# Gated attention and low-rank mixer: quartering the odd small matmuls, loads moved behind the first x + h's turn, scores over two PSUM tiles, other cover pairs, a last store in two

## The chip, the cores and the metric

One core of one Trainium2 chip. The metric is the device time of one execution in microseconds (us), as the median of several runs. The core has TensorE (PE, matrix products into PSUM), VectorE (DVE), ScalarE (ACT), GpSimd (POOL), and SyncE (SP), whose queue here issues all transfers. Each engine works through its instructions in the order in which they were written.

## What is computed

```python
batch, seq, d_model = (8, 3136, 256); d_qk = 64; rank = 32
# first part, for each batch
attn = np.maximum((1.0 / S) * np.matmul(z, z.transpose(0, 2, 1)), 0.0) ** 2
x = u * np.matmul(attn, v)
# second part
h = x.transpose(0, 2, 1) @ U @ V
u2 = x + h.transpose(0, 2, 1)
out = u2 + np.maximum(u2 @ w_ch1, 0.0) @ w_ch2        # w_ch1 256x1024, w_ch2 1024x256
```

## The kernel before, in words

The sequence of 3136 is cut into 24 full tiles of 128 rows and one of 64 (`NF` = 24, `NT` = 25). Full tiles come in six groups of four (512 rows, `NQ` = 6); the 64 rows are a seventh, small group (`NG` = 7). An item is a pair (batch, group); there are 56, and the loop over `t` gives each a slot. In slot `t` the attention of item `t` runs, x + h of the item seven back (`u2_unit`), and both layers of the item eight back (`ch1_part`, `ch2_stream`). `t == NG` is the slot of item (1, 0), the first in which the low-rank product of batch 0 (`t1_all`) and x + h occur.

All arithmetic of TensorE is in bfloat16 with float32 sums. The reduction of most products is cut into two halves of 64 rows, h = 0 and 1, that lie on the two halves of the array: `pair` (line 179) issues the two matmuls, each into another PSUM bank. A stream (`Ways`, line 616) does all its matmuls in one assignment of halves to banks, then in the other; between the two, `post` (line 170) has GpSimd hand on the semaphore that says that the other half has done with the bank. Line 184, the one in `pair`, therefore stands for nearly all matmuls in the profile. Four PSUM tiles of two banks each exist (`ps0` to `ps3`).

- Scores (`score_pairs`): z is held transposed twice over (`zzT`); two key tiles by 512 columns make a pair, rectified and squared into a block (`blk`). ScalarE mostly rectifies (L399) and VectorE squares (L364). Half of the blocks are mirror images, made by a transposing transfer (`issue_turn`, L421 and L429). At the very start the first two pairs (`rectify`, way "half", L376 to L381) are shared: ScalarE takes one bank, VectorE the other, of the same PSUM tile.
- The small group: `score_small`, and `av_small` (L714), the 64 rows' product with v on four quarters of the array, with 25 key tiles over two column halves. `t1_all` (L797) sums U times x over 25 tiles on four column strips of 32. `u2_unit` gives x + h; for the small group it is one matmul on half of the array.
- x + h is rounded to bfloat16 (L886) and turned by a transposing transfer (`x_turn`, L785) into `u2T`, which the first layer reads (L184, `ps<-u2T,w_bf`). The rectified result (L959 on VectorE, L962 on ScalarE) feeds the second layer (`ps<-w_bf,blk`).
- In the small group's slot there is no attention stream to fill waits. The second layer's stream runs in two halves, with score pairs or `av_small` between them as cover (`late`, line 1444).

The order of the work is planned in Python by a clock of its own (`clock`, `book`, `hold`, in units of a 256-column pair): `hold(due, f)` puts off loads, casts and squares, and `emit` (line 1110) mixes queues of units into a light stream, by places in that stream. SP issues transfers in the order planned; each also waits for the one eight before it. Loads of slot `t` (`load_part` for the next batch, `first_loads` for U, V and the two weights) are held to places in the slot up to `t == NG`; their casts run in the slot after it. `todo` spreads the score jobs over the slots. The last group's output is stored in two parts (`ch2_halves`, L1068, L1069).

Of the kernel before, what the change touches and what calls it, by code (L numbers as in the profile page):

```python
# [18 lines left out]
def kernel(  # L19
# [85 lines left out]
    ways = ["half", "half", "both", "dve"]  # L105
# [260 lines left out]
    def rectify(dst, src, b, part=1, whole=False):  # L366
# [3 lines left out]
        if whole and slot[0] == 0:  # L370
# [4 lines left out]
            if way == "half":  # L375
                nc.scalar.activation(out=dst[:, 0], in_=src[:, 0], func=AF.Relu, scale=scale)  # L376
                nc.vector.tensor_scalar(  # L377
                    out=dst[:, 1], in0=src[:, 1], scalar1=scale, scalar2=0.0, op0=ALU.mult, op1=ALU.max
                )
                nc.scalar.activation(out=dst[:, 0], in_=dst[:, 0], func=AF.Square)  # L380
                nc.vector.tensor_tensor(out=dst[:, 1], in0=dst[:, 1], in1=dst[:, 1], op=ALU.mult)  # L381
                done = max(book("act", ready, 5.2), book("dve", ready, 6.2))
                return done, max(book("act", ready, 5.2), book("dve", ready, 3.5))
# [156 lines left out]


# [161 lines left out]
    def av_small(b, g):  # L703
# [7 lines left out]
        for jt in range(NT):  # L711
            c = jt % 2
            for h in range(2):
                nc.tensor.matmul(  # L714
                    out=ps[c * hp : c * hp + rows, h, :D],
                    lhsT=smalls[b][h * hp : (h + 1) * hp, place_of(jt), :],
                    rhs=v_bfs[b][h * hp : (h + 1) * hp, jt, :],
                    start=(jt < 2),
                    stop=(jt >= NT - 2),
                    tile_position=(h * hp, c * hp),  # L720
                )
# [70 lines left out]
    def t1_all(b):  # L792
        k, pt = take_ps()
        for g in range(NG):
            for q, it, rows in tiles_of(g):
                c = it % NREP
                nc.tensor.matmul(  # L797
# [4 lines left out]
                    stop=(it + NREP >= NT),  # L802
                    tile_position=(0, c * R),
                )
        pe(8)
# [17 lines left out]
    def u2_unit(b, g, turn=True):  # L823
# [20 lines left out]
        else:  # L844
# [4 lines left out]
                        0,  # L849
                        0,  # L850
                        dict(
                            out=ps[:, 0, :D],
                            lhsT=V4_bf[:hp, t0 * P : (t0 + 1) * P],
                            rhs=t1s[b][:hp, :],
# [3 lines left out]
                    )  # L858
                ],
                D,  # L860
# [9 lines left out]
        nc.vector.tensor_tensor(out=o[:rows, :n, :], in0=four(ps)[:rows, :n, :], in1=x, op=ALU.add)  # L870
# [167 lines left out]
    def ch2_halves(b, g):  # L1038
# [3 lines left out]
        for a in range(2):  # L1042
            box = {}

            def step(i, way, first, least, a=a, box=box):
# [19 lines left out]
                if least == NH:  # L1065
                    ps_free[box["k"]] = book("dve", clock[0] + 3, 6.4)
                    o = u2s[b, g][:, 2 * a : 2 * a + 2, :]
                    nc.vector.tensor_tensor(out=o, in0=box["ps"][:, :, :D], in1=o, op=ALU.add)  # L1068
                    nc.sync.dma_start(out=rows_of(out[b])[:, g0 + 2 * a : g0 + 2 * a + 2, :], in_=o)  # L1069
                    queued(GW // 2)  # L1070
# [135 lines left out]
    def load_V(i0):  # L1206
# [30 lines left out]
        6: lambda: load_w(1),  # L1237
# [76 lines left out]
    score_burst(jobs0[:1])  # L1314
    score_burst(jobs0[1:2])
# [4 lines left out]
    for b in range(B):  # L1320
        for g in range(NQ):
            t = b * NG + g - 1
            new = jobs_of(b, g)
            if g == 0 and b > 0:
                x, y = (5, 10) if b == 1 else (5, 11)
# [18 lines left out]
    def early(b, g):  # L1344
        return b > 1 and g == NQ

    for t in range(n_items):
# [11 lines left out]
        if t > NG and g_now == NQ and b_next < B:  # L1359
            hold(clock[0] + 60 + 70, lambda b=b_next: load_u(b, NQ))  # L1360
        if t == n_items - 3:
            xTs[direct] = take_block()[1][:, : GT // 2, :].rearrange("p a (q d c) -> p (a q) d c", d=ND, c=P)
            x_turn(*direct, xTs[direct])
        for i, f in enumerate(casts_next):
            hold(clock[0] + (90 if g_now == NQ and b_next > 1 else 60 if t == NG else 15 if t >= NQ else 45) + 12 * i, f)
# [4 lines left out]
        steps += first_loads[t]() if t in first_loads else []  # L1370
# [4 lines left out]
        for i, f in enumerate(steps):  # L1375
            if t > NG:
                load(f)
            else:
                hold(clock[0] + 5 + 22 * i, lambda f=f: load(f))
        if t <= NG:  # L1380
            hold(clock[0] + 60, lambda t=t: load_u(*items[t + 1]))
# [35 lines left out]
        elif av:  # L1417

            if mix:
                qc += [(x, 1 - way, False, lambda way=way: ch1_small(*mix, way, box1)) for way, x in ((0, 36), (1, 48))]  # L1420
            if fin:
# [109 lines left out]
```

## Time and profile before

| | |
|---|---|
| Time, median of 3 runs | 983.55 us (982.08 to 983.84) |
| Profiled execution | 986.39 us, of it 984.6 from the first to the last instruction (span) |
| PE / DVE / ACT / POOL busy | 99% / 64% / 49% / 2% of the span |
| Granted TensorE clock, mean | 0.998 |
| DMA | 176.37 MB, 179 GB/s on the average |
| Chain that ended last | PE 96%, of it line 184 93% of the span; DMA of u2T 1% |

Each matmul row of the profile gives the start, the duration, the lines and the tiles; matmuls overlap, so the time from one start to the next is the slot that it takes, while its duration also holds its way through the array. "idle before <- releaser" is how long an engine stood and for whom. The granted clock is the share of full speed that TensorE was given.

### The profile page before, as it was taken

Reading aid. Unit: us, or ns where it says so; the run is one execution under the profiler, and the core shown is the slowest. Engines: PE = TensorE matmul, PEld = TensorE weight load, DVE = VectorE, ACT = ScalarE, POOL = GpSimd, SP = SyncE. Lnnn points to the kernel's source line nnn. Section 1 sums busy time; section 2 is a strip of 40 time slices with the busy share of each in tenths; the row PEclk is TensorE's granted clock in tenths of the full one; section 3 lists DMA queues with packets and bytes.
Section 4 is the critical chain, followed back from the end, with each engine's and each line's share of the span. In section 5 each row is a group of like instructions: output and inputs, shape, how many; then the busy total and the mean of one; then the engine's idle time right before and its main releaser. Section 6 shows DMA issues by size and latency. Waiting matters only on the chain.

```text
span 984.6 us, 35373 instructions
## 1 busy us (share of the span) xinstructions
PE 973.7 (99%) x16163; PEld 773.4 (79%) x16163; DVE 628.2 (64%) x811; ACT 482.4 (49%) x565; POOL 15.2 (2%) x25
## 2 busy tenths in 40 slices
PE   8999899999999999999999999999999999999998
PEld 5788677877778778787777877788777887778766
DVE  6878755668556685566755667556775567653363
ACT  7877642456324473355633555334654346431353
POOL 4200000000000000000000000000000000000000
PEclk9999999999999999999999999999999999999999
DMA  8899999979997799987999879997799978965153
GB/s 269 193 225 192 228 196 188 223 153 197 195 204 167 160 192 192 205 170 170 185 208 207 154 178 179 223 189 153 173 207 206 194 144 163 186 135 95 55 114 99
DMA packets 372405, 176.37 MB, mean 179 GB/s; under 512 B 347296, under 2 KB 350624, under 8 KB 372256
## 3 DMA queue, kind: packets, MB, share of 16 engines
q1 hardware_dynamic: 372256, 174.12, 85.6%
q8 instruction: 126, 2.06, 0.9%
q14 instruction: 23, 0.19, 0.1%
HBM read 62.56 MB, written 25.69 MB: 90 GB/s over the span
## 4 chain that ended last, share of the span: by engine, by line
PE 96%; DVE 1%; ACT 1%; DMA 1%; issue 0%; DVEq 0%
PE ps L184 93%; PE ps L714 1%; DMA u2T<-x_bf 1%; PE ps L797 1%; ACT blk L399 0%; PE ps L1096 0%; DVE blk L364 0%; PE ps L1300 0%; PE ps L331 0%; DVE blk L377 0%; DVE blk L381 0%; DVE x_bf L749 0%; DVE blk L406 0%; DVE out_sb L870 0%; DVE blk L395 0%
## 5 line engine op out<-in xcount | busy, mean ns | idle before, releaser
L184 PEld LDWEIGHTS <-blk 64*128 64x128 bf16 x12288 | 609.7, 94 | 159.9 <-POOLq L174 9.6
L184 PE MATMUL ps<-v_bf,blk 64*128 64x256 bf16 x9216 | 613.0, 269 | 2.3 <-DVE blk L364 1.1
L399 ACT ACTIVATE blk<-ps 128x1024 bf16<-128x1024 f32 (+1 forms) x335 | 315.3, 970 | 346.6 <-PE ps L184 343.2
L364 DVE TENSOR_TENSOR blk<-blk 128x1024 bf16<-128x1024 bf16 x350 | 221.1, 656 | 49.1 <-ACT blk L399 48.4
L184 PE MATMUL ps<-u2T,w_bf 64*128 64x512 bf16 (+1 forms) x1792 | 227.9, 350 | 2.8 <-DMA u2T<-x_bf 2.8
L184 PE MATMUL ps<-w_bf,blk 64*128 64x256 bf16 x3072 | 192.0, 269 | 0.0
L959 DVE TENSOR_SCALAR blk<-ps 128x1024 bf16<-128x1024 f32 x105 | 128.5, 1224 | 97.6 <-PE ps L184 96.6
L962 ACT ACTIVATE blk<-ps 128x1024 bf16<-128x1024 f32 x87 | 88.3, 1022 | 119.0 <-PE ps L184 118.8
L184 PE MATMUL ps<-zzT 64*128 64x512 bf16 (+2 forms) x902 | 129.8, 327 | 0.6 <-ACT zzT L340 0.6
L184 PEld LDWEIGHTS <-w_bf 64*128 64x128 bf16 x1792 | 84.3, 94 | 30.2 <-POOLq L174 5.0
L749 DVE TENSOR_TENSOR x_bf<-ps,u_sb 128x1024 bf16<-128x1024 f32 x48 | 58.7, 1222 | 71.4 <-PE ps L184 71.4
L870 DVE TENSOR_TENSOR out_sb<-ps,x_bf 128x1024 f32<-128x1024 f32 x42 | 51.4, 1224 | 58.1 <-PE ps L184 58.1
L1082 DVE TENSOR_TENSOR out_sb<-ps,out_sb 128x1024 f32<-128x1024 f32 x42 | 51.4, 1224 | 18.6 <-PE ps L184 18.3
L184 PEld LDWEIGHTS <-zzT 64*128 64x128 bf16 x902 | 41.2, 94 | 6.9 <-ACT zzT L340 1.5
L184 PE MATMUL ps<-t_sb,V_bf 64*128 64x256 bf16 x200 | 20.6, 269 | 0.0
L395 DVE TENSOR_SCALAR blk<-ps 128x1024 bf16<-128x1024 f32 (+1 forms) x14 | 16.6, 1185 | 5.9 <-PE ps L184 5.1
L206 DVE CAST v_bf<-stage 128x1024 bf16<-128x1024 f32 (+1 forms) x30 | 18.5, 617 | 0.0
L184 PE MATMUL ps<-v_bf,last_sb 64*128 64x256 bf16 x192 | 18.5, 269 | 0.0
L204 ACT CAST v_bf<-stage 128x1024 bf16<-128x1024 f32 (+1 forms) x18 | 18.1, 1005 | 0.0
L206 DVE CAST x_bf<-out_sb 128x1024 bf16<-128x1024 f32 x22 | 15.2, 689 | 0.3
L1082 DVE TENSOR_TENSOR blk<-ps,blk 128x1024 f32<-128x1024 f32 x5 | 6.1, 1225 | 11.9 <-PE ps L184 11.8
L204 ACT CAST x_bf<-out_sb 128x1024 bf16<-128x1024 f32 x13 | 13.5, 1037 | 0.0
(83 smaller groups left out, 239.1 us busy)
## 6 DMA issues: line engine op xcount, KB each, us to landing
u_sb<-in_u_dram SPq DMA_DIRECT2D x48, 512.0 KB, 5.1
stage<-in_v_dram SPq DMA_DIRECT2D x42, 512.0 KB, 6.1
out_dram<-out_sb SPq DMA_DIRECT2D x42, 512.0 KB, 3.1
stage<-in_z_dram SPq DMA_DIRECT2D x7, 512.0 KB, 5.9
blk<-in_v_dram SPq DMA_DIRECT2D x5, 512.0 KB, 6.3
out_dram<-blk SPq DMA_DIRECT2D x5, 512.0 KB, 2.6
blk<-blk SPq DMA_TRANSPOSE x156, 5.1
blk<-in_moe_w_ch_dram SPq DMA_DIRECT2D x4, 512.0 KB, 4.9
```

The costliest lines, as they stand in the source:

```text
L184: ins = nc.tensor.matmul(**args)
L204: nc.scalar.copy(out=out, in_=in_)
L206: nc.vector.tensor_copy(out=out, in_=in_)
L364: nc.vector.tensor_tensor(out=a, in0=a, in1=a, op=ALU.mult)
L395: nc.vector.tensor_scalar(out=dst, in0=src, scalar1=scale, scalar2=0.0, op0=ALU.mult, op1=ALU.max)
L399: nc.scalar.activation(out=dst, in_=src, func=AF.Relu, scale=scale)
L714: nc.tensor.matmul(out=ps[c * hp : c * hp + rows, h, :D], lhsT=smalls[b][h * hp : (h + 1) * hp, place_of(jt), :], rhs=v_bfs[b][h * hp : (h ...
L749: nc.vector.tensor_tensor(out=xs[b, g][:rows, :n, :], in0=four(box["ps"])[:rows, :n, :], in1=u_sbs[b, g][:rows, :n, :], op=ALU.mult,)
L870: nc.vector.tensor_tensor(out=o[:rows, :n, :], in0=four(ps)[:rows, :n, :], in1=x, op=ALU.add)
L959: nc.vector.tensor_single_scalar(out=r, in_=ps[:, :, :gw], scalar=0.0, op=ALU.max)
L962: nc.scalar.activation(out=r, in_=ps[:, :, :gw], func=AF.Relu)
L1082: nc.vector.tensor_tensor(out=o, in0=acc, in1=o, op=ALU.add)
```

## The change

Eight edits.

1. `av_small`: the 25th key tile is split by columns over both column halves: four matmuls of 128 columns instead of two of 256. `t1_all`: the 25th tile is split into four strips of 64 columns, one for each column strip of the array. `u2_unit`, small group: two matmuls of 128 columns on the two halves of the array instead of one of 256 on one half; the sum reads both banks.
2. The first two score pairs (`shared_pairs`) lie over two PSUM tiles, so that ScalarE reads only one and VectorE only the other.
3. Loads of the slots up to `t == NG`: U, V and weights ahead of the next batch's v; w2 is loaded in slot 7 instead of 6; at `t == NG` all loads are held to place 78 and later, and the next u to 88; at `t == NQ` the next u is loaded at place 5 instead of 60. So z of batch 2, w2 and u stand behind the first turn in SP's queue. Casts of the slot after follow at 45.
4. Batch 1's `av_small` is done in slot `NG`, at place 64, instead of as cover in slot 13; its u comes ahead for that.
5. Batches 2 to 7: two more of the first group's scores are left for the small slot.
6. Small slot: x + h of the small group comes first, then the first layer's eight parts, then a score pair; two score pairs, not one, lie between the halves of the second layer.
7. The last group's second store is split in two, the adds too; the second half goes out from ScalarE's queue.
8. Way "half" goes away.

```diff
...
     ready_turns = []
     urgent = []
     slot = [0]
-    ways = ["half", "half", "both", "dve"]
+    ways = ["both", "dve"]
     waiting = [0]
     def needed(e):
...
             ends = {"dve": dve + DVE, "act": act + 19, "both": max(act + 8.7, dve) + 7.5}
             given = bool(ways)
             way = ways.pop(0) if ways else min(ends, key=lambda w: ends[w])
-            if way == "half":
...
             if way == "dve":
                 if not given:
                     run_held(ready + 9)
...
         score_finish(score_pairs(jobs))
+    def shared_pairs(jobs):
+
+        (ka, a), (kb, d) = take_ps(), take_ps()
+        for i, (b, g, (J, h)) in enumerate(jobs):
+            zzT = zzTs[b]
+            if h == 0:
+                blocks[b, g, J] = take_block()
+            for jj in range(2):
+                key = J * GT + 2 * h + jj
+                nc.tensor.matmul(
+                    out=(a if jj == i else d)[:, jj, :],
+                    lhsT=half(zzT, jj, key * P, P),
+                    rhs=half(zzT, jj, groups[g][0], GW),
+                    start=True,
+                    stop=True,
+                )
+            pe(GW / 256)
+            dst = blocks[b, g, J][1][:, 2 * h : 2 * h + 2, :]
+            x, y = dst[:, i], dst[:, 1 - i]
+            nc.scalar.activation(out=x, in_=a[:, i], func=AF.Relu, scale=scale)
+            nc.vector.tensor_scalar(out=y, in0=d[:, 1 - i], scalar1=scale, scalar2=0.0, op0=ALU.mult, op1=ALU.max)
+            nc.scalar.activation(out=x, in_=x, func=AF.Square)
+            nc.vector.tensor_tensor(out=y, in0=y, in1=y, op=ALU.mult)
+            ps_free[ka] = book("act", clock[0] + 3, 5.2)
+            ps_free[kb] = book("dve", clock[0] + 3, 6.2)
+            book("act", 0, 5.2)
+            book("dve", 0, 3.5)
+
+            def finish(key=(b, g, J)):
+                squared[key] = squared.get(key, 0) + 1
+
+            hold(max(free_at["act"], free_at["dve"]), finish)
+
     def place_of(jt):
         if jt == NF:
...
         for jt in range(NQ + 1):
             while (b, jt) not in v_cast:
                 run_held(min(h[0] for h in held))
-        for jt in range(NT):
+        for jt in range(NT + 1):
             c = jt % 2
+            part = slice(0, D) if jt < NF else slice(c * D // 2, (c + 1) * D // 2)
+            at = min(jt, NF)
             for h in range(2):
                 nc.tensor.matmul(
-                    out=ps[c * hp : c * hp + rows, h, :D],
-                    lhsT=smalls[b][h * hp : (h + 1) * hp, place_of(jt), :],
-                    rhs=v_bfs[b][h * hp : (h + 1) * hp, jt, :],
+                    out=ps[c * hp : c * hp + rows, h, part],
+                    lhsT=smalls[b][h * hp : (h + 1) * hp, place_of(at), :],
+                    rhs=v_bfs[b][h * hp : (h + 1) * hp, at, part],
                     start=(jt < 2),
-                    stop=(jt >= NT - 2),
+                    stop=(jt >= NF),
                     tile_position=(h * hp, c * hp),
                 )
         pe(NT / 2 + 2)
...
         for g in range(NG):
             for q, it, rows in tiles_of(g):
                 c = it % NREP
+                if it == NF:
+                    break
                 nc.tensor.matmul(
                     out=pt[c * R : (c + 1) * R, 0, :D],
                     lhsT=U_bf[:, it, :],
                     rhs=xs[b, g][:, q, :],
                     start=(it < NREP),
-                    stop=(it + NREP >= NT),
+                    stop=False,
                     tile_position=(0, c * R),
                 )
-        pe(8)
+        for c in range(NREP):
+            part = slice(c * D // NREP, (c + 1) * D // NREP)
+            nc.tensor.matmul(
+                out=pt[c * R : (c + 1) * R, 0, part],
+                lhsT=U_bf[:, NF, :],
+                rhs=xs[b, NQ][:, 0, part],
+                start=False,
+                stop=True,
+                tile_position=(0, c * R),
+            )
+        pe(7)
         up = pool.tile([P, D], FP32, name="t1_up", bufs=1)
         t1 = pool.tile([P, D], BF16, name="t1_sb")
...
                 k,
                 [
                     (
-                        0,
-                        0,
+                        h,
+                        h,
                         dict(
-                            out=ps[:, 0, :D],
-                            lhsT=V4_bf[:hp, t0 * P : (t0 + 1) * P],
-                            rhs=t1s[b][:hp, :],
+                            out=ps[:, h, : D // 2],
+                            lhsT=V4_bf[h * hp : (h + 1) * hp, t0 * P : (t0 + 1) * P],
+                            rhs=t1s[b][h * hp : (h + 1) * hp, h * D // 2 : (h + 1) * D // 2],
                             start=True,
                             stop=True,
                         ),
                     )
+                    for h in range(2)
                 ],
-                D,
+                D // 2,
             )
         x = xs[b, g][:rows, :n, :]
         if b == B - 1:
...
         else:
             o = pool.tile([P, GT, D], FP32, name="out_sb", bufs=3)
         done = ps_free[k] = book("dve", clock[0] + 3, 11.2 * n / GT)
-        nc.vector.tensor_tensor(out=o[:rows, :n, :], in0=four(ps)[:rows, :n, :], in1=x, op=ALU.add)
+        if n == GT:
+            nc.vector.tensor_tensor(out=o, in0=four(ps), in1=x, op=ALU.add)
+        else:
+            apart = lambda a: a[:rows, 0, :].rearrange("p (c d) -> p c d", c=2)
+            nc.vector.tensor_tensor(out=apart(o), in0=ps[:rows, :, : D // 2], in1=apart(x), op=ALU.add)
         u2s[b, g] = o
         if not turn:
             return
...
                     post(box["k"])
                 if least == NH:
                     ps_free[box["k"]] = book("dve", clock[0] + 3, 6.4)
-                    o = u2s[b, g][:, 2 * a : 2 * a + 2, :]
-                    nc.vector.tensor_tensor(out=o, in0=box["ps"][:, :, :D], in1=o, op=ALU.add)
-                    nc.sync.dma_start(out=rows_of(out[b])[:, g0 + 2 * a : g0 + 2 * a + 2, :], in_=o)
+                    o = u2s[b, g]
+                    for q, n in ((0, 1), (1, 1)) if a else ((0, 2),):
+                        t = 2 * a + q
+                        nc.vector.tensor_tensor(
+                            out=o[:, t : t + n, :], in0=box["ps"][:, q : q + n, :D], in1=o[:, t : t + n, :], op=ALU.add
+                        )
+                        (nc.scalar if q else nc.sync).dma_start(
+                            out=rows_of(out[b])[:, g0 + t : g0 + t + n, :], in_=o[:, t : t + n, :]
+                        )
                     queued(GW // 2)
             units.append(Ways(NH, 0, step, box).units)
...
         3: lambda: load_V(0),
         4: lambda: load_V(2),
         5: lambda: load_w(0),
-        6: lambda: load_w(1),
+        NG: lambda: load_w(1),
     }
...
     clock[0] = 43
     free_at.update(dve=46, act=47)
     jobs0 = jobs_of(0, 0)
-    score_burst(jobs0[:1])
-    score_burst(jobs0[1:2])
+    shared_pairs(jobs0[:2])
     score_burst(jobs0[2:3])
     clock[0] = 60
...
             t = b * NG + g - 1
             new = jobs_of(b, g)
             if g == 0 and b > 0:
-                x, y = (5, 10) if b == 1 else (5, 11)
+                x, y = (5, 10) if b == 1 else (5, 9)
                 todo[t - 2] += new[:x]
                 todo[t - 1] += new[x:y]
                 todo[t] += new[y:12] if b == 1 else new[y:]
...
     direct = (B - 1, 0)
     def early(b, g):
-        return b > 1 and g == NQ
+        return b > 0 and g == NQ
     for t in range(n_items):
         slot[0] = t
...
             load_u(*items[t + 1])
         if t > NG and g_now == NQ and b_next < B:
             hold(clock[0] + 60 + 70, lambda b=b_next: load_u(b, NQ))
+        if t == NG:
+            hold(clock[0] + 2, lambda: load_u(1, NQ))
         if t == n_items - 3:
             xTs[direct] = take_block()[1][:, : GT // 2, :].rearrange("p a (q d c) -> p (a q) d c", d=ND, c=P)
             x_turn(*direct, xTs[direct])
         for i, f in enumerate(casts_next):
-            hold(clock[0] + (90 if g_now == NQ and b_next > 1 else 60 if t == NG else 15 if t >= NQ else 45) + 12 * i, f)
+            hold(clock[0] + (90 if g_now == NQ and b_next > 1 else 45 if t == NG + 1 else 15 if t >= NQ else 45) + 12 * i, f)
         casts_next = []
         spare += spare_next
         spare_next.clear()
         steps = load_part(b_next, g_now) if b_next < B else []
-        steps += first_loads[t]() if t in first_loads else []
+        steps = (first_loads[t]() if t in first_loads else []) + steps
         def load(step):
             casts_next.extend(step())
...
             if t > NG:
                 load(f)
             else:
-                hold(clock[0] + 5 + 22 * i, lambda f=f: load(f))
+                hold(clock[0] + (78 + 12 * i if t == NG else 5 + 22 * i), lambda f=f: load(f))
         if t <= NG:
-            hold(clock[0] + 60, lambda t=t: load_u(*items[t + 1]))
+            hold(clock[0] + (5 if t == NQ else 88 if t == NG else 60), lambda t=t: load_u(*items[t + 1]))
         if g_now == 0 and t:
             last_turn(att[0])
         if b_next < B and g_now == 2:
...
             if mix:
                 qc += [(x, 1 - way, False, lambda way=way: ch1_small(*mix, way, box1)) for way, x in ((0, 36), (1, 48))]
+            if t == NG:
+                qc.append((64, 2, False, lambda: av_small(1, NQ)))
             if fin:
                 qc.append((72, 2, False, lambda: (ch2_small(*fin), av_small(att[0], NQ))))
             k = min(2, len(mine) // 3)
...
                 c0, c1, d0, d1, c2, c3, d2, d3 = parts(mix, box1)
                 up = [lambda: u2_unit(*u2i)]
                 if fin:
-                    late = mine[-1:] if early(*att) else []
+                    late = mine[-2:] if early(*att) else []
                     rest = mine[: len(mine) - len(late)]
-                    order = [c0] + rest[:1] + [c1, d0, d1] + [c2] + rest[1:] + [c3, d2, d3] + up
+                    order = up + [c0, c1, d0, d1, c2, c3, d2, d3] + rest
                 else:
                     order = up + [small, c0, c1, d0, d1, c2, c3, lambda: t1_all(att[0]), d2, d3]
             qc += [(0, 0, False, f) for f in order]
```

## What was predicted, before the changed kernel had run

> **What bounds the kernel now.** I read the busy table first, then the chain of waits, then the stretches of time in which TensorE stood still, then the rows around each edit.
>
> ```profile
> PE 973.7 (99%) x16163; PEld 773.4 (79%) x16163; DVE 628.2 (64%) x811; ACT 482.4 (49%) x565; POOL 15.2 (2%) x25
> ```
>
> TensorE works 973.7 of 984.6 us and is 96% of the chain. Only two things can gain: fewer matmul slots, or the 10.9 us in which it stands. The largest hole, in the view of stretches (columns: stretch; length; busy us of PE, PEld, DVE, ACT, POOL; granted clock; DMA share; GB/s):
>
> ```profile
> 108.70:111.40 2.70, 0.00 (x0) 0.00 (x0) 2.03 (x3) 0.00 (x0) 0.00 (x0) 0.95 0.74 135
> ...
> 112.40:113.40 1.00, 1.00 (x14) 0.69 (x12) 0.00 (x0) 0.00 (x0) 0.00 (x0) 0.50 1.24 283
> ...
> 114.40:115.40 1.00, 1.00 (x18) 0.73 (x14) 0.00 (x0) 0.87 (x2) 0.00 (x0) 0.93 0.66 172
> ```
>
> After 2.76 us without a matmul the clock is 0.50 for three microseconds and 0.93 in the next: 3 x 0.50 + 0.07 = 1.57, about 1.55 us of it lost while working. The mean clock, 0.998 of 984.6 us, says that nearly no other clock was lost. What was late, from the DMA queue's timeline:
>
> ```profile
> 99.10 0.78 SPq L226 DMA_DIRECT2D stage<-in_z_dram  x1
> ...
> 100.39 0.50 SPq L226 DMA_DIRECT2D stage<-in_z_dram  x1
> 100.94 1.09 SPq L308 DMA_DIRECT2D u_sb<-in_u_dram  x2
> 102.97 2.25 SPq L785 DMA_TRANSPOSE u2T<-x_bf  x1
> ```
>
> and of tile u2T, all its turns:
>
> ```profile
> DMA to landing us min/median/max: 2.3/3.6/8.4
> ```
>
> This first turn of x + h is the 8.4: it went out at 102.97, as soon as its cast was done, behind 2.3 MB of loads (z 512 and 256 KB, w2 512, u 2 x 512), and landed at 111.41. Small slots (columns: start, duration):
>
> ```profile
> 439.81 0.53 PE L184 MATMUL ps<-zzT 64*128 64x64 bf16 x24
> 440.16 0.19 PE L591 MATMUL ps<-zzT 64*128 64x64 bf16 x1
> ...
> 458.28 0.84 PE L797 MATMUL ps<-x_bf,U_bf 128*32 128x256 bf16 x24
> 458.95 0.27 PE L797 MATMUL ps<-x_small,U_bf 128*32 128x256 bf16 x1
> 459.15 1.05 PE L184 MATMUL ps<-v_bf,blk 64*128 64x256 bf16 x16
> ```
>
> 24 matmuls of t1 go in six rounds of four, (458.95 - 458.28) / 6 = 0.11 us each; the 25th has a round alone. Twelve pairs with 64 columns take 0.35, 0.029 each: a short pair costs its columns. The small slot of a batch:
>
> ```profile
> 453.12 0.27 PE L184 MATMUL ps<-w_bf,blk 64*128 64x256 bf16 x1
> 453.23 2.00 PE L184 MATMUL ps<-w_bf,blk 64*128 64x256 bf16 x31
> 455.06 0.38 PE L184 MATMUL ps<-zzT 64*128 64x512 bf16 x2
> 455.34 1.92 PE L184 MATMUL ps<-w_bf,blk 64*128 64x256 bf16 x32
> 457.10 0.27 PE L184 MATMUL ps<-v_bf,blk 64*128 64x256 bf16 x2
> ```
>
> The second 32 take 1.76 us (0.11 a pair). The first 32 and one lone small matmul take 1.94, so 1.94 - 1.76 - 0.11 = 0.07 is a wait; the score pair takes 0.28 where 16 pairs of 512 columns before it (449.66 to 453.12) take 0.216 each: 0.06 more.
>
> **The change, part by part.**
>
> *Loads behind the first turn.* In the changed order, z, w2 and one u load come behind the turn in SP's queue. Ahead of it stay, from the slot before, one u load (512 KB, some 8 us earlier), the attention tail's turn, 64 KB of u and a turn of four tiles (1.45 us on the queue in its old place). The cast's own chain on VectorE (L810, L811, two squares, L395, L870, L886) is unchanged, so the turn goes out at 102.97 and lands near the median, at 106.6. The batch-1 tail product, moved here, adds 13 rounds (1.33 us) ahead of the first use, which moves from 108.7 to 110.0. Gain 2.76 + 1.55 = 4.3; bounds: 0, if a wait as long comes back, and 4.4. I take 4.3, since the landing has 3.4 us to spare.
>
> What this moves: w2's two casts go from ScalarE (1.05 each) to VectorE (0.68 each), in a queue where squares and the next x + h stand behind them. The loads go out at about 105.3 and land, by w2's own row (4.9 to 5.2), near 111; the casts' turn comes near 115, the first use near 126. The tail product's four small VectorE operations (0.17 + 0.68 + 0.42 + 0.42 = 1.7) come in 104 to 108, where VectorE had squares nearly without a break until 106.9. So the product with u (L749, 1.22) ends near 111.4 and its PSUM tile is wanted at 111.7: 0.3 spare, and 0 to 1 us if that is gone. I take 0. The reordered loads of slots 2 to 5 cost nothing: the one turn that now stands behind four more V loads (2.8 us on the queue) and a u load (0.6) went out at 60.5, will near 64, lands 5.1 later (median of its row), and is read at 85. U, V and w1 are first used after 95.
>
> *Odd matmuls split.* Per batch: the attention tail's last half-full round, 256 columns to 128, saves 0.055; t1's lone one, 256 to 64, 0.08; the lone x + h one, 256 to 128 in a pair, 0.055. 0.19 x 8 = 1.5. The 0.20 from the lone matmul to the next kind, 0.09 over a round, stays. Were the pieces to run one after another, they would cost 4 x 0.055, 4 x 0.029 and 2 x 0.055 in place of 0.11 each: 0.12 more per batch, 0.9 in all. Between -1.5 and +0.9 I take -1.4: the pairs at 0.029 run side by side.
>
> The Trainium skill (TensorE: Matmul & The Clock Gate, Back-to-back issue gap) speaks against it: with a weight load to each, 128 columns sustain about 81 ns a matmul, so by the page ten pieces would take some 0.8 us per batch and the edit would lose about 3.9 us, an estimate from that page. The pairs at 0.029 us disagree with it.
>
> *Two cover pairs, u first.* In the six small slots of batches 1 to 6 the lone matmul goes ahead of the first layer, one score pair ahead of the second, and two pairs between its ways. That gives the last rectification 0.2 us more and the hand-over 0.43 in place of 0.28: 0.13 x 6 = 0.8 (bounds 0 and 1). The last first-layer tile's chain is in front of no other wait: VectorE's 1.23 for the previous store ends 0.4 before the accumulator is wanted.
>
> *Pairs over two PSUM tiles.*
>
> ```profile
> 6.13 0.69 DVE L377 TENSOR_SCALAR blk<-ps 128x512 bf16<-128x512 f32 x1 [2.29 <-ACT blk L376]
> ...
> 8.00 0.86 DVE L381 TENSOR_TENSOR blk<-blk 128x512 bf16<-128x512 bf16 x1
> ```
>
> VectorE waited for ScalarE to have read its half of the same tile. With a tile for each, it starts near 5.3; but the second job's matmuls now wait for the first readers (about 6.0 and 6.1, were at 5.1). The four halves, ready at 6.75, 7.27, 7.90, 8.86, come at about 6.75, 6.45, 7.7, 8.0; TensorE's transposes at 9.24 then wait for GpSimd's cast (ends 8.59). Gain 0.6 there; later loads and casts can take some back: 0.5, bounds -0.2 and 0.9.
>
> *Last store halved.*
>
> ```profile
> 979.91 1.27 DVE L1068 TENSOR_TENSOR blk<-ps,blk 128x512 f32<-128x512 f32 x2
> 980.62 1.01 SPq L1069 DMA_DIRECT2D out_dram<-blk  x2
> ```
>
> The last add, 0.63, becomes two of 0.42 (as L1082's small one), so its second half goes out 0.2 later, with 128 KB in place of 256, on ScalarE's queue, where nothing stands behind it. Stores land 2.3 (256 KB) and 2.0 (64 KB) after issue: -0.3 + 0.2 = -0.1, bounds +0.4 and -0.4.
>
> Sum: 4.3 + 1.4 + 0.8 + 0.5 + 0.1 = 7.1 us. The profiled execution took 986.39 (span 984.6 and 1.8 around it), 2.84 above the median 983.55; the sum makes it 979.3, and the median 976.4.
>
> **Rivals.**
>
> *The wait moves to the second turn.* Before, it went out at 122.80 and was wanted at 132.44. Now it is wanted near 129.3, its cast ends near 120.7, and the z, w2 and u loads that were issued ahead of the first turn now stand between the two, 2.3 MB issued from 105 on in place of 99. At 3.6 to 8.4 to land it comes at 124 to 131. For: the same bytes have less time. Against: DMA share was 0.34 at 118 to 120, so there was room. Price up to 2 us without loss of clock (the 0.85 us hole near 27 us lost none): 978.4; a hole of 2.7 costs 4.3 and gives 980.7. Chance 0.16.
>
> *The pieces run one after another*: 7.1 - 1.4 - 0.9 = 4.8, 978.7; were each as dear as a whole round, seven rounds more a batch, 6.2 in all, 984.0. For: no row has four quarters with so few columns. Against: the 0.029. Chance 0.05, of it 0.01 at the far end. The Trainium skill's 81 ns, by the estimate above, would give 981.7.
>
> *Slower: w2's load holds VectorE.* The cast waits in order, squares, x + h and rectifications stand behind it, and TensorE stops with its clock halved. It costs a microsecond for each by which the load lands after about 118, and 1.55 more once the hole is 2.7. To pass 983.55 it must be over 5.5 late, landing after 123, 18 us after issue; the slowest u load took 9.1. About 986. Chance 0.04.
>
> **How the numbers follow.** Forecast 0.75, and the three rivals 0.16, 0.05 and 0.04. What can be told from no change is 0.2%, 2.0 us: faster is below 981.6. All of the forecast, 0.12 of the first rival and 0.04 of the second: 0.91; their far ends, 0.04 and 0.01: the same, 0.05; slower 0.04. Range: the best bounds, 4.4 + 1.5 + 1.0 + 0.9 + 0.4 = 8.2, give 975.3; the runs shown lie up to 1.5 below their median, so 974.0. Upward it takes in the first two rivals: 980.6.
>
> **What would show it.** Right: no TensorE wait for u2T, clock 1.00 from 100 to 130, the first turn landing in under 6 us; t1's last four within 0.04 of each other and the next kind 0.1 sooner; no 0.28 score pair in the small slots; VectorE's first score at 5.3. Wrong: a hole over 0.5 us between 103 and 135, a clock under 1.00 there, or VectorE idle before a w2 cast.

## The result, and the profile after

The changed kernel took 980.32 us (median of 13 runs, 979.08 to 981.98), the kernel before beside it 982.89 (13 runs, 981.55 to 986.07): a ratio of 0.9968, 95% interval 0.9958 to 0.9977, so 2.3 to 4.1 us less. Forecast were 976.4 and 7.1 less: the direction held, the size did not. That 980.32 lies just inside the range given, 974.0 to 980.6, is luck: its upper end had been opened for the two rivals, and neither came. Four later sets of both kernels gave ratios of 0.9977 to 0.9982, that is 1.8 to 2.3 us less.

The two profiled executions, however, differ by just that: 986.39 and 979.08, spans 984.62 and 977.30. The way between them, by the starts of the first matmul of `t1_all` in batches 0 and 1 and of the last matmul:

| stretch, us | before, profiled | before, profiled once more | changed, profiled | changed, four more profiles |
|---|---|---|---|---|
| start to t1 of batch 0 | 95.67 | 95.51 | 94.95 | 94.61 to 95.87 |
| t1 of batch 0 to t1 of batch 1 | 122.96 | 119.24 | 118.27 | 118.27 to 118.94 |
| t1 of batch 1 to the last matmul | 761.46 | 761.45 | 759.53 | 759.53 to 760.10 |
| from there to the end | 4.53 | 4.53 | 4.54 | 4.55 to 4.56 |

The second column is an experiment below. The stretch with the first turn of x + h was 3.72 us longer in the one execution that the forecast was read from than in the next one of the same kernel; everything behind it agrees within 0.01. Of the 7.3 us between the two profiled executions, 4.7 lie in that stretch, 1.9 behind it and 0.7 ahead of it. The 0.7 is within what the start varies by itself in the last column, so that the sum of 7.1 fits these two so well is in part luck.

The busy table of the changed kernel:

```profile
PE 969.4 (99%) x16211; PEld 774.7 (79%) x16211; DVE 633.7 (65%) x815; ACT 480.0 (49%) x562; POOL 15.7 (2%) x25
```

The same three stretches as before, in the same columns:

```profile
108.70:111.40 2.70, 2.70 (x48) 2.13 (x44) 2.35 (x4) 0.72 (x2) 0.00 (x0) 1.00 1.05 383
112.40:113.40 1.00, 1.00 (x18) 0.61 (x14) 1.00 (x2) 0.00 (x0) 0.00 (x0) 1.00 0.95 342
114.40:115.40 1.00, 1.00 (x17) 0.66 (x14) 1.00 (x3) 0.72 (x2) 0.00 (x0) 1.00 1.13 334
```

No hole, and the clock stays at 1.00. SyncE's queue, and the landing of all turns of x + h:

```profile
102.27 1.23 SPq L811 DMA_TRANSPOSE u2T<-x_bf  x1
103.56 0.58 SPq L1239 DMA_DIRECT2D blk<-in_moe_w_ch_dram  x1
104.19 0.53 SPq L308 DMA_DIRECT2D u_sb<-in_u_dram  x1
104.77 0.43 SPq L1239 DMA_DIRECT2D blk<-in_moe_w_ch_dram  x1
105.25 1.00 SPq L226 DMA_DIRECT2D stage<-in_z_dram  x2
...
117.85 1.97 SPq L220 DMA_DIRECT2D stage<-in_z_dram  x2
```

```profile
DMA to landing us min/median/max: 3.0/3.7/6.7
```

The turn goes ahead of w2, u and z, as forecast, and landed after 3.1 us (the 6.7 is that of a later turn, near 578 us). The last line of the queue is new: the tails of batch 2's z went out at 106.81 before, and go out 11 us later now. The small slot (start, duration):

```profile
446.90 0.39 PE L184 MATMUL ps<-zzT 64*128 64x512 bf16 x2
447.11 1.92 PE L184 MATMUL ps<-w_bf,blk 64*128 64x256 bf16 x32
448.86 0.60 PE L184 MATMUL ps<-zzT 64*128 64x512 bf16 x4
449.29 1.92 PE L184 MATMUL ps<-w_bf,blk 64*128 64x256 bf16 x32
...
452.89 0.20 PE L835 MATMUL ps<-x_small,U_bf 128*32 128x64 bf16 x4
453.03 1.05 PE L184 MATMUL ps<-v_bf,blk 64*128 64x256 bf16 x16
```

Each 32 of the second layer take 1.75 us, pairs of scores 0.21: no wait is left there. t1's last four pieces and the way to the next kind take 0.14, where the lone matmul took 0.20.

### The profile page after: what moved, and what is told of

Its sections match the earlier page's. It is cut to its first block, busy times and chain, and to the rows that moved or that the text cites. A ratio compares the mean times of both kernels' runs of the same rounds, so it can differ in the third digit from the quotient of the medians.

```text
span 977.3 us, 35450 instructions
## 1 busy us (share of the span) xinstructions
PE 969.4 (99%) x16211; PEld 774.7 (79%) x16211; DVE 633.7 (65%) x815; ACT 480.0 (49%) x562; POOL 15.7 (2%) x25
## 4 chain that ended last, share of the span: by engine, by line
PE 98%; DVE 1%; ACT 0%; issue 0%; DVEq 0%
PE ps L184 95%; PE ps L740 1%; PE ps L825 1%; PE ps L1145 0%; ACT blk L390 0%; DVE blk L364 0%; PE ps L1349 0%; PE ps L331 0%; DVE blk L553 0%; DVE blk L397 0%; DVE x_bf L775 0%; ACT last_sb L390 0%; DVE blk L1113 0%; PE ps L542 0%; DVE blk L761 0%
## 5 line engine op out<-in xcount | busy, mean ns | idle before, releaser
L1002 DVE TENSOR_SCALAR blk<-ps 128x1024 bf16<-128x1024 f32 x111 | 135.9, 1224 | 103.7 <-PE ps L184 102.8
L184 PE MATMUL ps<-w_bf,blk 64*128 64x256 bf16 x3072 | 189.8, 269 | 0.0
L1005 ACT ACTIVATE blk<-ps 128x1024 bf16<-128x1024 f32 x81 | 82.2, 1022 | 123.9 <-PE ps L184 120.1
L184 PEld LDWEIGHTS <-w_bf 64*128 64x128 bf16 x1792 | 82.2, 94 | 27.9 <-POOLq L174 5.2
L206 DVE CAST v_bf<-stage 128x1024 bf16<-128x1024 f32 (+1 forms) x35 | 21.5, 615 | 0.0
L386 DVE TENSOR_SCALAR blk<-ps 128x1024 bf16<-128x1024 f32 x14 | 17.1, 1223 | 6.5 <-PE ps L184 5.8
L184 PE MATMUL ps<-t_sb,V_bf 64*128 64x256 bf16 (+1 forms) x208 | 20.3, 265 | 0.0
L204 ACT CAST x_bf<-out_sb 128x1024 bf16<-128x1024 f32 x19 | 19.7, 1037 | 0.0
L204 ACT CAST v_bf<-stage 128x1024 bf16<-128x1024 f32 x13 | 13.5, 1040 | 0.0
L626 ACT ACTIVATE attn_small<-ps 128x512 bf16<-128x512 f32 (+1 forms) x32 | 13.1, 499 | 0.0
```

The source lines that it names most:

```text
L184: ins = nc.tensor.matmul(**args)
L204: nc.scalar.copy(out=out, in_=in_)
L206: nc.vector.tensor_copy(out=out, in_=in_)
L386: nc.vector.tensor_scalar(out=dst, in0=src, scalar1=scale, scalar2=0.0, op0=ALU.mult, op1=ALU.max)
L626: nc.scalar.activation(out=dst[:, jj], in_=src[:, jj], func=AF.Relu, scale=scale)
L1002: nc.vector.tensor_single_scalar(out=r, in_=ps[:, :, :gw], scalar=0.0, op=ALU.max)
```

## Experiments: was the late turn usual?

Both kernels again, unchanged.

> The kernel before, unchanged, to see how it runs from one execution to the next. The thirteen runs of it known so far go from 981.55 to 986.07, and the profiled one was the highest, 986.39. Theory A (the late turn is rare): the hole of 2.76 us and its half clock belong to the highest runs; most executions have a granted clock of 1.000 and lie at 981.5 to 983.5, and a second profile shows no wait of TensorE for u2T, or one under 1 us. Theory B (the late turn is usual): the clock is 0.998 in most executions, the second profile shows a hole of 2 to 3 us there, and the changed kernel gives 4 us back somewhere.

> The changed kernel again, for a second profile. Theory A: as in its first profile no wait of TensorE between 90 and 140 us, 980.3, clock 1.000. Theory B: its first profile, 979.08, was a lucky one, and in this one TensorE stands 2 to 4 us somewhere after the first turn.

The kernel before took 982.37 (11 runs, 981.75 to 983.24), and 982.07 in the 33 runs beside them. From its list of waits (us in total, times, longest), and the landing of its turns:

```profile
PE ps L184 <- DMA u2T<-x_bf: 0.5, 1, 0.5
```

```profile
DMA to landing us min/median/max: 2.3/3.4/6.2
```

The first turn landed after 6.2 us, not 8.4; TensorE stood 0.54 us, and no clock was lost. The turn follows the last load ahead of it. That load landed at 108.21 here and at 110.53 in the first profile, the turn at 109.03 and 111.41, and in all seven profiles with the old order of loads, those below included, the turn landed 0.8 to 0.9 us behind that load. Between these two profiles SyncE makes the difference: it came through the attention tail's turn (L554) at 97.9 instead of 99.0, so the loads went out over a microsecond earlier, while the turn went out at 102.82 instead of 102.97. That is not the only cause, for in one profile below (a_oldloads) SyncE was through at 97.5 and TensorE still stood 1.25 us.

So the wait as such is usual. Six profiles have the old loads and nothing added ahead of the turn: it landed after 6.2 to 8.4 us in all of them, and TensorE stood 0.54, 0.77, 0.89, 1.25, 1.55 and 2.76 us. Only the 2.76 came with a lower clock. Over all sets the kernel before ran 167 times: median 982.43, ten runs at 984 or more, three over 986. For 154 of these runs the granted clock is on record: it was 0.998 in the two of them over 986, and 0.999 or 1.000 in all others. The execution that was profiled first, 986.39 with 0.998, is of that rare kind. The changed kernel took 980.65 (979.09 to 982.47), and its profile has one new wait of 0.34 us at 125.10 (of it below). Theory A holds for the kernel before, with the wait of under 1 us that it allowed.

To have the long wait at will, two loads that nothing reads, each 512 KB of w2 into a free block, were put ahead of the turn of the kernel before (b_more2):

```diff
+        if t == NG:
+            for i in range(2):
+                hold(clock[0] + 30 + i, idle_load)
```

> The kernel before with two more loads of 512 KB, whose data nothing reads, ahead of the first turn of x + h. If that turn lands when the bytes ahead of it are through: at 380 GB/s 1 MB takes 2.7 us more, the wait of 0.5 us in the kernel's usual execution becomes 2.5 to 3.5, the clock falls to half behind it, 0.998 in most runs, and the time rises by 3 to 5 us, to what the first profiled execution had (986.4). Rival: the turn's landing does not go by the loads ahead of it; then the time rises by under 1 us.

It took 987.36 us (984.76 to 988.28, 6 runs), ratio 1.0043 (1.0029 to 1.0057). Two of the runs lie at 984.8 and 985.1 with a clock of 1.000, four at 986.7 to 988.3 with 0.996 to 0.998. Stretches of its profile, columns as above:

```profile
109.00:110.00 1.00, 0.00 (x0) 0.00 (x0) 0.47 (x1) 0.00 (x0) 0.00 (x0) 1.00 2.24 82
110.00:111.00 1.00, 0.00 (x0) 0.00 (x0) 1.00 (x2) 0.00 (x0) 0.00 (x0) 1.00 0.54 123
...
113.00:114.00 1.00, 1.00 (x14) 0.73 (x12) 0.00 (x0) 0.87 (x1) 0.00 (x0) 0.53 1.26 284
114.00:115.00 1.00, 1.00 (x12) 0.54 (x8) 0.00 (x0) 0.42 (x2) 0.00 (x0) 0.50 0.66 106
```

The turn landed after 8.8 us, TensorE stood 3.16, and the clock fell to half. The mechanism and its price were read rightly; how long the wait usually is was not.

## Experiments: what the new order of loads does

The order of loads and casts (part 3 of the change, without the tail product) in the kernel before (b_loads), and the changed kernel with parts 3 and 4 undone (a_oldloads):

```diff
-        6: lambda: load_w(1),
+        NG: lambda: load_w(1),
...
-                hold(clock[0] + 5 + 22 * i, lambda f=f: load(f))
+                hold(clock[0] + (78 + 12 * i if t == NG else 5 + 22 * i), lambda f=f: load(f))
...
-            hold(clock[0] + 60, lambda t=t: load_u(*items[t + 1]))
+            hold(clock[0] + (5 if t == NQ else 88 if t == NG else 60), lambda t=t: load_u(*items[t + 1]))
```

> The kernel before with the new order of loads and casts alone; the tail product of batch 1 stays where it was. Theory A: 0 to 1.2 us less at the median, ratio 0.9988 to 1.000, and the highest runs (over 984) are gone. Theory B: 4.3 less, ratio 0.9956, unless the gain is given back inside this part, and then the profile has a new wait.

> The changed kernel with the loads, the casts and the tail product of batch 1 back in their old places; the other edits stay. Theory A: 0 to 1.2 us over the changed kernel at the median, 980.3 to 981.5, and 2.2 to 3 below the one before; some runs 3 to 4 higher, with a clock of 0.998. Theory B: 4.3 over the changed kernel, 984.6.

The order alone made the kernel slower: 983.64 (983.08 to 984.39), ratio 1.0014 (1.0005 to 1.0023), which neither theory had. There is no wait for u2T, but on TensorE, and on ScalarE ahead of it:

```profile
122.32 0.93 PE L184 MATMUL ps<-v_bf,blk 64*128 64x256 bf16 x14
124.25 1.49 PE L184 MATMUL ps<-w_bf,blk 64*128 64x256 bf16 x24 [1.00 <-ACT blk L399]
126.07 0.61 PE L184 MATMUL ps<-w_bf,blk 64*128 64x256 bf16 x8 [0.34 <-DVE blk L959]
```

```profile
119.27 1.04 ACT L399 ACTIVATE blk<-ps 128x1024 bf16<-128x1024 f32 x1
122.60 0.67 ACT L204 CAST z_bf<-stage 128x576 bf16<-128x576 f32 x1 [2.30 <-DMA stage<-in_z_dram]
123.18 1.93 ACT L399 ACTIVATE blk<-ps 128x1024 bf16<-128x1024 f32 x2
```

The cast with 576 columns reads the last tile of z too, the tail of 64 rows. ScalarE stood 2.30 us and VectorE 3.27 for it, and the rectifications behind the cast came late, so their PSUM tile did. The tails (L220) left SyncE from 119.55 on there, behind a turn that took 7.56 us on its queue. In the changed kernel's five profiles the same cast is waited for 0.3 to 1.3 us on ScalarE, 1.3 to 2.3 on VectorE, and TensorE stands 0 to 0.34. Without parts 3 and 4 it is 981.00 (980.11 to 983.69; ratio 0.9991, 0.9982 to 0.9999) against the 980.65 (0.9982, 0.9973 to 0.9991) of the same set. So these parts bring 0.35 us at the median and 0.9 by the ratios, whose intervals overlap; 4.3 is out. Nor is it all the first turn's: the profile without these parts has a wait of 1.25 us for that turn, but also 0.50 us of waits near 210 us, which the old place of the tail product brings (below).

That the tails are the cause was tested by sending them right behind z, in the kernel with the new order alone (b_loads_tails) and in the changed kernel (a_tails, a_tails2; a_again2 and a_again3 are the changed kernel on the same chips):

```diff
-                hold(clock[0] + 75, tails)
+                hold(clock[0] + (5 if b == 2 else 75), tails)
```

> The kernel before with the new order of loads, and with batch 2's four tail transfers right behind its z. The new order without this cost 1.3 us over the kernel before (983.64, its profile with TensorE waits of 1.00 and 0.34 us near 124). Theory C (those waits are the late tails'): they are gone, 1.3 less than that, so 0 to 0.6 below the kernel before, ratio 0.9994 to 1.000, and without runs over 984. Rival: another load is behind it (w2, whose casts moved to VectorE), and the 1.3 stay.

It took 982.24 (981.68 to 982.84), ratio 0.9995 (0.9986 to 1.0004), and with no wait on either cast:

```profile
119.30 1.04 ACT L399 ACTIVATE blk<-ps 128x1024 bf16<-128x1024 f32 x1
120.21 0.68 ACT L204 CAST z_bf<-stage 128x576 bf16<-128x576 f32 x1
120.77 1.05 ACT L399 ACTIVATE blk<-ps 128x1024 bf16<-128x1024 f32 x1
```

From 1.0014 to 0.9995, each against the kernel before on the same chip: the loss was the tails'. The order as such then gives 0.4 us at the median, with an interval that includes no gain, and none of the 11 runs is over 983.

> The changed kernel once more, beside the next one on the same chip. Its 24 runs so far lie at 979.1 to 982.5, median 980.4, while its two profiled ones were 979.08 and 979.54. Theory C (the late tails): the second z cast of batch 2 waits for the four small tail transfers behind the long turn on the load queue; where they are late, ScalarE, VectorE and then TensorE stand near 123 to 126 us, 0 to 3 us of it. The median stays near 980.4. Theory D: the spread comes from the first 15 us, where the first loads land; then the profiles differ there only.

> The changed kernel with one edit: the four tail transfers of batch 2 go out right behind its z, ahead of u, v and the long turn, instead of some 12 us after it. Theory C: neither engine waits for the second z cast, the median falls by 0.8 to 1.3 us against the changed kernel on this chip, to about 979.3, and the runs over 981 are gone. Theory D: no change, within 0.3 us.

> The changed kernel, to compare the next two with on one chip: median 980.3 to 980.7, as before.

> The changed kernel with batch 2's tail transfers right behind its z, again. If the late tails are what its median has lost: 0.5 to 1.0 below the changed kernel, near 979.7, and fewer runs over 981. Otherwise within 0.3 of it.

The changed kernel with early tails took 979.59 (5 runs) against 980.33, then 980.37 (12 runs) against 980.63; the ratios to the kernel before are 0.9970 and 0.9977 against 0.9977 and 0.9979. Runs over 981 became rare (1 of 17; 13 of 58 of the changed kernel in all its sets), but the median moved by less than was expected, 0.3 in the larger set. Most of what sets the changed kernel's median over its best runs is something else.

## Experiments: the other parts, one by one

In the kernel before, the odd matmuls split alone (b_pack), and the small slot's order and cover pairs alone (b_cover), as they stand in the diff.

> The kernel before with the odd matmuls split alone. If the pieces run side by side: a batch takes 119.83 - 0.19 = 119.64 us, and 1.4 us less in all, ratio 0.9986. If they run one after another, 0.9 more, ratio 1.0009.

> The kernel before with the small slot's new order and the two cover pairs alone. From the stages (119.83 us a batch before, 119.71 with the odd matmuls split, 119.50 changed): 0.21 a batch, 119.62, six times, 1.3 less, ratio 0.9987. My forecast had 0.13 a batch and 0.8.

The odd matmuls split gave 981.39 (980.49 to 983.27), ratio 0.9989 (0.9981 to 0.9998), and a batch 119.71 us. The new cover gave 983.19 (981.73 to 984.27), ratio 1.0005 (0.9996 to 1.0014), although a batch fell to 119.67. In the one slot that still has the tail product as its cover, that of batch 1, new waits came up:

```profile
207.79 0.71 PE L184 MATMUL ps<-zzT 64*128 64x512 bf16 x4
208.76 0.39 PE L184 MATMUL ps<-zzT 64*128 64x512 bf16 x2 [0.26 <-ACT blk L962]
209.40 1.92 PE L184 MATMUL ps<-w_bf,blk 64*128 64x256 bf16 x32 [0.24 <-DVE blk L959]
```

With all score pairs put behind the first layer, their PSUM tiles and the last rectification of VectorE are waited for, 0.50 us together. The changed kernel with its old loads, where that product was back in this slot too, had the same two waits. So part 6 without part 4 pays 0.50 us in that slot, and the two have to be costed together.

The first two score pairs over two PSUM tiles, alone (b_start), the changed kernel without them (a_oldstart), and the same with early tails (a_tails_oldstart):

> The kernel before with the first two score pairs over two PSUM tiles alone. As forecast: 0.5 us less, VectorE's first score near 5.3 us where the first load comes at its usual time. Rival: the second job's wait and later loads take it back, within 0.2 us of before; or the PSUM tiles taken in another order cost up to 0.2.

> The changed kernel with the first two score pairs over one PSUM tile, as before. Alone, the two tiles brought nothing at the median (982.60 against 982.71), though t1 of batch 0 began 0.5 us earlier in the profile: the first turn was waited for 0.2 us longer. If the gain is taken back there, it counts in the changed kernel, where that turn is not waited for: 0.5 over the changed kernel, 980.9. Rival: the gain is within the spread of the first loads' landing, and the time is the changed kernel's, 980.4, within 0.2.

> The same with the first two score pairs over one PSUM tile, as before. If the start's gain counts where nothing later waits: 0.5 over a_tails2. If it is lost in the landing of the first loads: within 0.2 of a_tails2.

Alone they gave 982.60 (982.04 to 987.02), ratio 1.0007 (0.9996 to 1.0018). Three of these 12 runs lie at 985.96 to 987.02 with a clock of 0.998, while only three of 167 of the kernel before lie over 985.9. With the old loads the long wait seems to come more often behind this start, which no run followed up. Without them the changed kernel took 980.17 (979.75 to 981.06), ratio 0.9976 (0.9966 to 0.9986), with early tails 980.22 against 980.37. They bring nothing that the median shows. The profiles say why: t1 of batch 0 begins at 95.54 us on the average of the eleven profiled executions with them, at 95.62 of the nine without, but between 94.61 and 96.52 with them and 95.37 and 95.94 without. At the start the matmuls run at half speed, and the traces' clock record has its first entry, full speed, where that ends: at 3.8 to 6.8 us in 17 of the 20 profiles, at 9.5 to 10.0 in three of the eleven. These three begin t1 at 95.87 to 96.52 (96.23 on the average), the six others without blank matmuls (below) at 94.61 to 95.87 (95.13). So in these profiles the two tiles do bring 0.5 us on the average where the half speed ends early, and lose 0.6 where it ends late. Rows of a late one (a_tails2), and then of an early one of the changed kernel (a_again4):

```profile
6.24 0.61 PE L542 MATMUL ps<-zzT 64*128 64x512 bf16 x2 [0.81 <-DVE blk L553]
6.61 0.66 PE L184 MATMUL ps<-zzT 64*128 64x512 bf16 x2
7.04 1.09 PE L184 MATMUL ps<-v_bf,blk 64*128 64x256 bf16 x8
```

```profile
6.25 0.39 PE L542 MATMUL ps<-zzT 64*128 64x512 bf16 x2 [0.81 <-DVE blk L553]
6.46 0.39 PE L184 MATMUL ps<-zzT 64*128 64x512 bf16 x2
6.78 0.61 PE L184 MATMUL ps<-v_bf,blk 64*128 64x256 bf16 x8
```

TensorE waits 0.81 us between the two pairs. The theory was that this stop prolongs the half speed of the start; seven blank matmuls, put there, work through it (a_warm, and a_tails_warm with early tails; a_again4 is the changed kernel):

```diff
+            if i == 0:
+                kc, c = take_ps()
+                for _ in range(7):
+                    nc.tensor.matmul(out=c[:, 0, :P], lhsT=blank, rhs=blank, start=True, stop=True)
+                ps_free[kc] = clock[0]
```

> The changed kernel, to compare the next two with on one chip: median 980.3 to 980.7, most runs over 980.2 and some at 979.1 to 979.8.

> The changed kernel with seven matmuls of the blank tile between its first two score pairs, into a PSUM tile of their own, so that TensorE works in the 0.81 us in which it waits there. Theory E (the stop lets the half speed of the start go on to 9.5 us in many executions): the upper runs come down by 1.2 us, the median by 0.5 to 1.0, to 979.4 to 980.0. Rival: no change within 0.3, and the two groups of runs stay.

> The same with batch 2's tails early too. Theory E: 979.2 to 979.6, nearly all runs under 980. Rival: as a_tails2, 980.4.

The stop shrank to 0.13 us, and to 0.32 with early tails, but the time stayed: 980.33 and, with early tails, 980.18, against 980.35; ratios 0.9980 (0.9971 to 0.9989), 0.9978 (0.9969 to 0.9987) and 0.9978 (0.9969 to 0.9986). The gain that the theory promised did not come. A small one could not be seen: three late ends in nine, 1.1 us each, are under 0.4 us on the average, an estimate from the profiles above, and less than the intervals can tell.

Its mechanism, though, fits the traces. In their clock records all changes lie whole steps of 3.413 us apart, and where the steps begin differs from one execution to the next. In all 20 profiles the step at whose end full speed came holds 2.85 to 3.41 us of matmuls. In the three late ones the step before it holds 2.60 to 2.79, with most of the stop in it, and the half speed went on for that one step more. The two profiles with blanks turned to full speed at 5.86 and 4.56, so whether the blanks prevent a late end stays untested.

What else spreads the changed kernel's runs from 979.1 to 982.5 is open. Two of its 58 runs, 982.47 and 981.71, had a clock of 0.998 and 0.997; four of its five profiled executions lie under 979.8, where only 17 of its 58 runs do. No version was clearly faster than the changed kernel.

## Why the prediction was wrong, step by step

The step that failed is the term of 4.3 us for the first turn, and with it the line under the sum that carried the whole sum from the profiled execution, 986.39, to the median, 983.55. The profiled execution lay 2.84 over that median because of this very wait: what only that execution had cannot be taken from the median too. In the five other profiled executions with the old loads the wait was there, but it was 0.5 to 1.6 us long and cost no clock. Set against the runs:

| term | forecast | measured | by |
|---|---|---|---|
| first turn, loads behind it | 4.3 | 0.35 | parts 3 and 4 undone, same set (0.9 by the ratios) |
| odd matmuls | 1.4 | 1.0 | 119.83 - 119.71 = 0.12 a batch, eight times |
| cover, u first | 0.8 | 1.3 | 119.71 - 119.50 = 0.21 a batch, six times |
| start | 0.5 | 0.1 | 95.62 - 95.54 |
| last store | 0.1 | 0.0 | 4.53 to 4.54 from the last matmul to the end |
| sum | 7.1 | 2.7 | measured 2.57 by the medians, 3.15 by the ratio; 1.8 to 2.3 in the later sets |

- *First turn.* The mechanism, the order in the queue, the landing (3.1 us for 3.6) and the price of hole and clock were right, and the two loads ahead showed it. The term was mis-sized: it took the longest wait of six, with its half clock, for the usual one. The sign was 986.39, over all three runs shown. The landing of 8.4 beside a median of 3.6 was no such sign, since this turn lands after 6.2 to 7.2 us in the five other profiles too.
- *What is late next.* Forecast was that w2's casts could hold VectorE. They did not; the z tails, which the working followed nowhere, held both engines. The rule of that rival was right (a cast waits in order, and the work behind it with it), the transfer was another, and the price was 0 to 0.34 us of TensorE in the changed kernel's profiles, 1.34 where the order stood alone. The second turn, the likelier rival, was waited for in no profile.
- *Odd matmuls.* The tail product's last round gave 0.047 (forecast 0.055) and t1's 0.07 (0.08). The lone x + h, split alone, gave nothing where 0.055 was booked: before, it began 10 ns beside a matmul of the second layer on the other half of the array, and had no slot of its own. Four pieces start within 12 ns, so the rival that they run one after another is out. The Trainium skill's 81 ns a matmul of 128 columns (TensorE: Matmul & The Clock Gate, Back-to-back issue gap) would make 0.32 us of four, an estimate from that page; the trace disagrees, with 0.16 us from the first of the tail product's four to the next kind.
- *Cover.* 0.16 a batch alone (119.83 - 119.67) and 0.21 beside the split matmuls, for 0.13. The lone matmul's 0.11 us was counted as a slot, but was part of the wait, which was 1.94 - 1.76 = 0.18. And ahead of the first layer, where part 6 puts it, the lone matmul does take a slot, 0.109 us whole (b_cover) and 0.056 split: the 0.05 that the odd matmuls lacked is in this row. That part 6 needs part 4 was not seen.
- *Start.* VectorE began its first score at 5.32 us (5.1 to 5.5 in the five profiles), as forecast, and the second pair came at 6.06, as forecast too, after a stop of 0.81 us. The 0.5 us came where the half speed ended early; that the stop can make the half speed go on was not in the working.
- *Last store.* The same 3.0 us from SyncE's last issue to the end as before.

## What to carry to other kernels

Before a wait in a profile is booked as gain, ask whether the usual execution has it: set the profiled execution's time against the runs, and the late transfer against the same transfer in a second profile. Where the execution is an outlier, subtract its excess from that execution alone. Comparing the transfer with others of its kind does not answer this: the first turn was late in every profile, and only its last 1 to 2 us were rare. When loads move behind a critical transfer, follow every small transfer that belongs to them as well, down to the first instruction that reads it, and see what is queued behind that instruction. An edit that needs another one (cover pairs, once the tail product is out of the slot) should be costed with it and without it.

## What the hardware showed beyond that

- The wait's price has a step. Holes of 0.54 to 1.55 us ahead of the first turn's reader left the clock at full speed, holes of 2.76 and 3.16 were each followed by 3.41 us at half. Counted by the steps of 3.413 us in the clock record, up to 1.25 us idle within one step left it at full, while 2.07 and 2.43 were followed by one step at half.
- At the start the matmuls run at half speed (a pair of 512 columns 0.37 us apart in place of 0.21) while the granted clock's column stands at 1.00. The clock record has no entry before the change to full speed, so that this 1.00 is no measured clock. The half speed ended at 3.8 to 6.8 us in 17 profiles and at 9.5 to 10.0 in three, in which a step that held the stop of 0.81 us had 2.60 to 2.79 us of matmuls.
- Two transfers of 16 KB, the tails of z, held two engines for 2.3 and 3.3 us, because they stood behind one turn on SyncE's queue that took 7.56.
